# Attention and SwiGLU on one core: 7-for-8 block products for q, k and v, two-bank PSUM tiles, an accumulating residual and a planned engine order

## The chip, the cores and the metric

The kernel runs on one core of one Trainium2 chip. The metric is the device time of an execution in microseconds, as the median over runs. A core has TensorE (PE, matrix products into PSUM), VectorE (DVE), ScalarE (ACT), GpSimd (POOL) and SyncE (SP); the last three issue the transfers here.

## The reference, cut to what matters

S = 2048 rows, D = 1024, F = 3584, 32 heads of 32, all in bf16. Every row attends to 8 rows: itself and those 2, 4, ... 14 before it.

```python
xn  = layernorm(x)
q, k, v = split(xn @ wqkv)                       # [2048, 3 * 1024]
idx = pos[:, None] - 2 * arange(8)               # window 8, dilation 2
a   = softmax(where(idx >= 0, einsum(q, k[idx]) * 32**-0.5, -1e9))
s   = einsum(a, v[idx]).reshape(S, D) @ wo
g   = silu((silu(xn @ w1) * (xn @ w3)) @ w2)
return x + s * g
```

## The kernel before, in words

The rows go in two blocks b of 1024, each of two chunks c of 512; chunk c lies in half c % 2 of `xT` (the normalized rows, transposed, 8 tiles of 128 features by 512 rows) and of `qo` (q, later the attention output). One matmul multiplies a 128x128 weight tile with 128x512 and adds into one PSUM bank of 512 fp32 columns. All products go through `mm_prod` (L117), so that they carry line L120 in the profile and are told apart by the tile they write: qkv, ua / ue / ub (mlp_up), da / de / db (mlp_down), s (wo).

The stages of one block:

- `ln_transpose` (L191): loads x, layernorm, 32 transposes per chunk on TensorE (L182), evictions to `xT`.
- `qkv(c)` (L198): for each of q, k, v 2 MB of weights in two loads (L207) and 8 x 8 matmuls; ScalarE evicts each bank (L220), k and v into `kT` and `vT`, which hold one chunk and the 16 rows before it.
- `xn_sums` (L289): four sums of blocks of `xT`, kept in `xs`.
- `mlp_up` (L335): 14 blocks fb of 256 columns of w1 and w3. Gate and up of both chunks form a 2x2 block product, made with 7 block multiplications in place of 8 (7 x 2 x 4 = 56 matmuls per fb). It takes sums of weight blocks (`w_sums`, L326, made by VectorE in block 0, stored in `s_dram` and loaded again in block 1) and sums of partial products: `fork` (L128) copies a PSUM bank to another, `snap` (L134) copies one to SBUF, and VectorE adds (L374, L383) and multiplies (L397, L400). The last of the seven products is put off into the next fb as `tail` (L393), which `flush` runs.
- `attention(c)` (L229): on VectorE. For each window offset w q*k in two products of 128x2048 (L236), adds over feature groups (L238 to L240) into `E`; 32 transfers of 64 KB by GpSimd regroup E into `L` (L244); softmax in fp32 (L248 to L261); 32 transfers spread the weights over E again (L264); then PV (L272 to L287): products with `vT` and adds into the same half of `qo`.
- `mlp_down(b)` (L425): again a 2x2 block product with 7 multiplications, 392 matmuls; h sums s1 to s4 by VectorE (L463, L464, L478, L490), w2 sums (`w2_sums`, L411, made beside mlp_up of block 0) from `t_dram`.
- `wo(c)` (L525): 64 matmuls; per 128x512 piece a load of x (L538), product with the gate (L541), add (L542), and a store from ScalarE's queue (L543).

The driver (L545) orders them: for each b `qkv(c0)`, in block 1 then `wo(1)`, `xn_sums`, `mlp_up` over the first 11 (block 1: 10) fb, `attention(c0)`, `qkv(c1)`, the other fb, `attention(c1)`, `mlp_down`, `wo(c0)`; `wo(3)` comes last. Within it the framework sets each engine's order by program order, `tc.high_priority()` around operations that free banks, and `tc.issue_after` (L324), which holds weight sums behind a given operation. Pools give the buffers: 8 PSUM banks of [128, 512], `k2` with 8 slots, `r8` with 6 slots for weights, `att` with 3. SyncE's queue carries every load, GpSimd's the stores to scratch and the regrouping.

Of the kernel before, what the change touches and what calls it, by code (L numbers as in the profile page):

```python
# [2 lines left out]

# [5 lines left out]
FP32 = mybir.dt.float32  # L9
# [4 lines left out]
AX = mybir.AxisListType  # L14


@with_exitstack
def kernel(
# [49 lines left out]
    const = ctx.enter_context(tc.tile_pool(name="const", bufs=1))  # L68
    dram = ctx.enter_context(tc.tile_pool(name="dram", bufs=1, space=bass.MemoryType.DRAM))
    psum = ctx.enter_context(tc.tile_pool(name="psum", bufs=8, space=bass.MemoryType.PSUM))  # L70
    small = ctx.enter_context(tc.tile_pool(name="small", bufs=4))
    keep = ctx.enter_context(tc.tile_pool(name="keep", bufs=1))
    r8 = ctx.enter_context(tc.tile_pool(name="r8", bufs=6))
    att = ctx.enter_context(tc.tile_pool(name="att", bufs=3))
    k2 = ctx.enter_context(tc.tile_pool(name="k2", bufs=8))

    s_dram = dram.tile([FB, P, 4, KH, 2 * P], FP16, name="s_dram")
    t_dram = dram.tile([P, FH, 4, CH], FP16, name="t_dram")

# [29 lines left out]

    warm = k2.tile([P, CH], BF16, tag="k2", name="warm")  # L110
    nc.vector.memset(warm[:], 0.0)
    for i in range(8):
        wps = psum.tile([P, CH], FP32, tag="mm", name=f"warm{i}")
        for _ in range(2 if i < 4 else 1):
            nc.tensor.matmul(wps[:], lhsT=warm[:, 0:P], rhs=warm[:], start=True, stop=True)

    def mm_prod(ps, lhs, rhs, first):  # L117
        n = len(lhs)
        for k in range(n):
            nc.tensor.matmul(  # L120
                ps[:], lhsT=lhs[k], rhs=rhs[k], start=(first and k == 0),
                stop=(k == n - 1), skip_group_check=not first,
            )

    def bank(name):
        return psum.tile([P, CH], FP32, tag="mm", name=name)

    def fork(name, src):  # L128
        dst = bank(name)
        with tc.high_priority():  # L130
            nc.scalar.copy(out=dst[:], in_=src[:])  # L131
        return dst

    def snap(name, src):  # L134
        dst = k2.tile([P, CH], FP32, tag="k2", name=name)
        with tc.high_priority():
            nc.scalar.copy(out=dst[:], in_=src[:])
        return dst

    def ln_norm(c, sts, xt4):  # L140
        n = len(sts)
        mv = small.tile([P, n, nc.vector.BN_AGGR_DIM], FP32, tag="mv")
        rstd = small.tile([P, n], FP32, tag="rstd")
        for i, st in enumerate(sts):
            g = c * NST + st
            nc.sync.dma_start(out=xt4[:, st, :], in_=x_flat[g * P:(g + 1) * P, :])
            stats = small.tile([P, 2, nc.vector.BN_STATS_DIM], FP32, tag="stats")
# [11 lines left out]
    def ln_norm_act(c, sts, xt4):  # L159
        n = len(sts)  # L160
        v = small.tile([P, 4, n], FP32, tag="v")
# [8 lines left out]
        with tc.high_priority():  # L170
# [424 lines left out]
```

## Time and profile before

| | us |
|---|---|
| median of 3 runs (766.59 to 772.36) | 768.1 |
| span of the profiled execution | 766.9 |
| TensorE busy | 749.4 |
| VectorE busy | 602.1 |
| ScalarE busy | 321.1 |
| GpSimd busy | 97.2 |

The busy time of each engine in each stage, from the profile's table of windows (PE and DVE in us, DMA the mean busy share of the 16 DMA engines):

| window, us | stage | PE | DVE | DMA |
|---|---|---|---|---|
| 0 to 13.1 | layernorm and transposes of chunk 0 | 8.28 | 7.27 | 0.86 |
| 13.1 to 57.2 | qkv(0), transposes of chunk 1 | 44.10 | 28.26 | 0.59 |
| 57.2 to 190.8 | mlp_up(0), 11 fb, attention(0) | 133.28 | 117.67 | 0.79 |
| 190.8 to 239 | qkv(1) | 43.80 | 47.92 | 0.59 |
| 239 to 276.1 | mlp_up(0), 3 fb | 36.85 | 34.38 | 0.62 |
| 276.1 to 365.2 | mlp_down(0), attention(1) | 88.84 | 44.55 | 0.69 |
| 365.2 to 379 | wo(0) | 13.80 | 11.12 | 0.90 |
| 379 to 434.2 | qkv(2), wo(1) | 55.20 | 54.37 | 0.55 |
| 434.2 to 561.7 | mlp_up(1), 10 fb, attention(2) | 124.17 | 99.23 | 0.56 |
| 561.7 to 602 | qkv(3) | 40.30 | 32.20 | 0.40 |
| 602 to 650.7 | mlp_up(1), 4 fb | 48.70 | 39.59 | 0.59 |
| 650.7 to 735.1 | mlp_down(1), attention(3) | 84.40 | 59.59 | 0.56 |
| 735.1 to 767 | wo(2), wo(3) | 27.66 | 25.95 | 0.38 |

How to read it: the page's first part says which engine could bound the whole, its slices show where it does not work, the chain says what the end followed from, and the groups say what one operation lasts and what it waited for. Durations of one engine's neighbours overlap, so that the cost of one more operation is the distance between starts, which the timeline and the chain of work show. Transfers are given by line with the median from issue to landing.

### The profile page before, as it was taken

The page shows a single profiled execution, that of the slowest core. Times are in us where ns is not written, and L with a number is a line of the kernel's source. Part 1 is how long each engine was busy: PE and PEld are TensorE (multiplying, and loading weights), DVE is VectorE, ACT ScalarE, POOL GpSimd, SP SyncE. Part 2 cuts the span into 40 slices and gives each one's busy share as a digit, 9 for nine tenths or more (in the row PEclk, how much of TensorE's full clock was granted, in tenths as well). Part 3 has the DMA queues.
Part 4 walks back from the last instruction along what each step waited for, and adds up shares of the span by engine and source line. Part 5 has one row for each costly group of instructions (what it writes and reads, how often), then busy time and mean ns, then how long its engine had stood idle before and what let it go on. Part 6 is the DMA issues. An engine that isn't in the chain of part 4 may idle for free.

```text
span 766.9 us, 9404 instructions
## 1 busy us (share of the span) xinstructions
PE 749.4 (98%) x3516; PEld 375.6 (49%) x3516; DVE 602.1 (79%) x828; ACT 321.1 (42%) x534; POOL 97.2 (13%) x172
## 2 busy tenths in 40 slices
PE   7999999999899999999999899999999999999997
PEld 4664444444565444445566344444466544444443
DVE  6479988887998999150799998565995995924997
ACT  5536444654225489264033044464433444321200
POOL 0000042132000001413000004040000004040000
PEclk8999999999999999999999999999999999999999
DMA  9633799898753668658853836565535257464634
GB/s 331 217 111 108 234 302 272 275 285 297 261 189 83 218 227 268 172 190 262 261 179 103 270 114 169 175 195 165 187 115 201 98 172 207 157 196 147 200 100 140
DMA packets 123117, 150.56 MB, mean 196 GB/s; under 512 B 6080, under 2 KB 97728, under 8 KB 119488
## 3 DMA queue, kind: packets, MB, share of 16 engines
q1 hardware_dynamic: 110336, 115.36, 48.2%
q0 software_dynamic: 8128, 30.42, 11.7%
q10 hardware_dynamic: 4608, 4.20, 1.6%
q8 instruction: 27, 0.44, 0.3%
q14 instruction: 18, 0.15, 0.1%
HBM read 115.34 MB, written 26.21 MB: 185 GB/s over the span
## 4 chain that ended last, share of the span: by engine, by line
PE 86%; DVE 8%; DMA 4%; issue 1%; ACT 1%; SPq 0%; DVEq 0%; ACTq 0%
PE ub L120 18%; PE qkv L120 15%; PE ue L120 12%; PE ua L120 12%; PE db L120 9%; PE de L120 6%; PE da L120 6%; PE s L120 5%; DMA wt<-in_A_wqkv_dram 2%; DVE B L286 1%; DVE B L272 1%; DVE qo L287 1%; DVE p_t L236 1%; PE tp L182 1%; DVE C L272 1%
## 5 line engine op out<-in xcount | busy, mean ns | idle before, releaser
L120 PE MATMUL qkv<-xT,wt 128*128 128x512 bf16 x768 | 169.9, 383 | 4.9 <-DMA wt<-in_A_wqkv_dram 4.4
L120 PEld LDWEIGHTS <-wt 128*128 128x128 bf16 x768 | 110.1, 144 | 63.8 <-DMA wt<-in_A_wqkv_dram 5.8
L120 PEld LDWEIGHTS <-st 128*128 128x128 f16 x896 | 87.7, 98 | 107.4 <-issue 1.7
L120 PE MATMUL ua<-xT,w 128*128 128x512 bf16 x448 | 106.7, 381 | 2.9 <-ACT ub L131 2.9
L120 PEld LDWEIGHTS <-w 128*128 128x128 bf16 x672 | 65.9, 98 | 84.0 <-issue 5.9
L120 PE MATMUL ub<-xs,st 128*128 128x512 f16 x448 | 106.7, 381 | 0.0
L120 PEld LDWEIGHTS <-h_sb 128*128 128x128 bf16 (+1 forms) x672 | 65.5, 98 | 77.5 <-issue 0.5
L236 DVE TENSOR_TENSOR p_t<-qo,kT 128x2048 bf16<-128x2048 bf16 x64 | 77.5, 1215 | 8.5 <-ACT kT L220 8.5
L120 PE MATMUL db<-wt,h_sb 128*128 128x512 f16 x336 | 73.7, 379 | 0.0
L374 DVE TENSOR_TENSOR us<-ue,us 128x512 f32<-128x512 f32 x56 | 37.5, 685 | 38.3 <-PE ue L120 38.3
L120 PE MATMUL s<-wot,qo 128*128 128x512 bf16 x256 | 55.7, 379 | 0.0
L367 ACT ACTIVATE h_sb<-ua 128x512 bf16<-128x512 f32 x56 | 33.3, 598 | 53.3 <-PE ua L120 53.3
L385 ACT ACTIVATE sg<-us 128x512 bf16<-128x512 f32 x56 | 34.8, 630 | 46.7 <-DVE us L374 46.7
L120 PE MATMUL ub<-xs,w 128*128 128x512 f16 x224 | 53.4, 379 | 0.9 <-DVE h_sb L383 0.9
L120 PE MATMUL ue<-xs,st 128*128 128x512 f16 x224 | 52.9, 379 | 0.1
L120 PE MATMUL ue<-xT,st 128*128 128x512 bf16 x224 | 52.9, 379 | 0.0
L131 ACT COPY ub<-ua 128x512 f32<-128x512 f32 x56 | 31.6, 570 | 44.4 <-PE ua L120 25.4
L120 PE MATMUL da<-wt,h_sb 128*128 128x512 bf16 x224 | 49.2, 379 | 0.3 <-DMA wt<-in_B_w_dram 0.3
L264 POOL DMA_DIRECT2D E<-pb x64 | 36.8, 582 | 92.9 <-DVE pb L261 89.1
L397 DVE TENSOR_TENSOR h_sb<-h_sb,ub 128x512 bf16<-128x512 bf16 x56 | 37.0, 679 | 14.4 <-PE ub L120 14.4
L244 POOL DMA_DIRECT2D L<-E x64 | 37.0, 586 | 59.3 <-DVE E L240 55.6
L220 ACT CAST qo<-qkv 128x512 bf16<-128x512 f32 x32 | 18.6, 585 | 61.3 <-PE qkv L120 45.0
(103 smaller groups left out, 841.1 us busy)
## 6 DMA issues: line engine op xcount, KB each, us to landing
wt<-in_A_wqkv_dram SPq DMA_DIRECT2D x24, 1024.0 KB, 7.1
w<-in_B_w_dram SPq DMA_DIRECT2D x42, 512.0 KB, 5.1
s_dram<-st POOLq DMA_DIRECT2D x14, 1024.0 KB, 5.9
wt<-t_dram SPq DMA_DIRECT2D x16, 896.0 KB, 5.4
st<-s_dram SPq DMA_DIRECT2D x14, 1024.0 KB, 5.3
wt<-in_B_w_dram SPq DMA_DIRECT2D x12, 896.0 KB, 6.1
wot<-in_A_wo_dram SPq DMA_DIRECT2D x8, 1024.0 KB, 7.9
w2q<-in_B_w_dram SPq DMA_DIRECT2D x14, 512.0 KB, 3.8
```

The source lines that it names most:

```text
L120: nc.tensor.matmul(ps[:], lhsT=lhs[k], rhs=rhs[k], start=(first and k == 0), stop=(k == n - 1), skip_group_check=not first,)
L131: nc.scalar.copy(out=dst[:], in_=src[:])
L182: nc.tensor.matmul(tp[:, k * P:(k + 1) * P], lhsT=xt4[:, st, kt * P:(kt + 1) * P], rhs=ident[:], start=(k == 0), stop=(k == KH - 1), skip_ ...
L220: nc.scalar.copy(out=dst, in_=ps[:])
L236: nc.vector.tensor_mul(p_t[:], qT[:, jh * 4:jh * 4 + 4, :], kT[:, jh * 4:jh * 4 + 4, o:o + CH])
L244: nc.gpsimd.dma_start(out=L[r // 2][sq * 32:(sq + 1) * 32, r % 2, :, :], in_=E[r:P:NR, :, sq * P:(sq + 1) * P],)
L264: nc.gpsimd.dma_start(out=E[r:P:NR, :, sq * P:(sq + 1) * P], in_=pb[sq * 32:(sq + 1) * 32, :, :],)
L272: nc.vector.tensor_mul(dst, E[:, w, :].unsqueeze(1).to_broadcast([P, 4, CH]), vT[:, js, o:o + CH])
L367: nc.scalar.activation(out=h_sb[:, fl[i], 0:CH], in_=pa[i][:], func=ACTF.Silu)
L374: m = nc.vector.tensor_add(su2[i][:], pe[i][:], su2[i][:])
L385: nc.scalar.activation(out=sg2[i][:], in_=su2[i][:], func=ACTF.Silu)
L397: nc.vector.tensor_mul(h_sb[:, fl[i], 0:CH], h_sb[:, fl[i], 0:CH], pb[i][:])
```

## The change

1. *7 for 8 in q, k, v.* `group`, taken out of `mlp_up`, is used by `pair` for k and v in block 0 and for q, k and v in block 1, over both chunks at once; q of block 0 stays plain. Sums of the weights (`pair_sums`) are four VectorE operations of 128x2048 per matrix; those of k and v are stored in `sk_dram` and loaded again in block 1. The second chunk's k and v wait in `kv_dram` (block 0) or in `h_sb` (block 1, `park`) and are moved into `kT` and `vT` by GpSimd transfers once attention of the first chunk has used them. It is for fewer matmuls and for reading wqkv once per block.
2. *Two-bank tiles.* PSUM tiles become [128, 2, 512], four of them, and `k2` has 4 slots of twice the size; evictions, silus, adds and products take 1024 columns at once. The w2 sums are made two blocks at a time.
3. *Attention's regrouping through DRAM.* E goes to `e_dram` in two halves and comes back in 4 transfers each; p goes to `p_dram` in 4 transfers per half and returns with one that repeats each row 4 times. The z sums go by halves, and PV takes window offsets 0 to 3 for both feature halves, then 4 to 7.
4. *The residual.* `residual(c)` copies x to the output from DRAM to DRAM on SyncE's queue, ahead of the load of fb 6 of block 0. The wo pieces (128x1024) are multiplied with the gate in fp32, and GpSimd adds them to the output with an accumulating transfer. The last two pieces are done as before.
5. *wo(0) and the transposes of chunks 2 and 3 inside mlp_down(0)*: pieces of either follow single products of its last two multiplications.
6. *A planned order.* `Plan` reads the finished program, gives every instruction and transfer a cost, list-schedules them forward and backward six times, and adds order-only dependencies, so that VectorE, ScalarE and GpSimd run in the order planned; TensorE and SyncE keep the program's. `tc.high_priority` and `tc.issue_after` go.
7. *The driver*: see the end of the diff; CUT is (13, 10), so that attention(0) follows fb 12, and attention(1) fb 13.

The diff's core (`Plan`'s methods, mlp_down's evictions and the changes of names and pools left out):

```diff
+    def group(nm, a11, a12, a22, s, c11, c12, c22, c21):
+        s1, s2, s3, s4 = s
+        pa = bank(f"ua{nm}")
+        for i in I:
+            mm_prod(pa[:, i], a11[i], b11, True)
+        pe = bank(f"ue{nm}")
+        for i in I:
+            mm_prod(pe[:, i], s1[i], t1, True)
+        pb = fork(f"ub{nm}", pa)
+        sp5 = snap(f"us5{nm}", pe)
+        flush()
+        for i in I:
+            mm_prod(pa[:, i], a12[i], b21, False)
+        c11(pa)
+        for i in I:
+            mm_prod(pb[:, i], s2[i], t2, False)
+        su2 = snap(f"us2{nm}", pb)
+        for i in I:
+            mm_prod(pe[:, i], s4[i], b22, False)
+        c12(pe, su2)
+        for i in I:
+            mm_prod(pb[:, i], s3[i], t3, False)
+        c22(pb, sp5)
+
+        def tail():
+            for i in I:
+                mm_prod(pb[:, i], a22[i], t4, False)
+            c21(pb)
+        pend.append(tail)
...
+            def second(ps, part, js):
+                if later is None:
+                    nc.vector.tensor_add(d1[:, js, :], ps[:], part[:])
+                else:
+                    kv = k2.tile([P, 2, CH], BF16, tag="k2", name=f"kv{b}_{t}_{js.start}")
+                    nc.vector.tensor_add(kv[:], ps[:], part[:])
+                    nc.gpsimd.dma_start(out=kv_dram[later, :, js, :], in_=kv[:])
...
+        def gather(wh):
+            ws = slice(wh * 4, wh * 4 + 4)
+            nc.gpsimd.dma_start(out=e_dram[wh], in_=E[:, ws, :].rearrange("p w t -> p (w t)"))
+            for sq in range(4):
+                nc.gpsimd.dma_start(
+                    out=L[wh][sq * 32:(sq + 1) * 32],
+                    in_=e_dram[wh].rearrange("(h r) (w q t) -> h (r w) q t", r=NR, w=4, q=4)[:, :, sq, :],
+                )
...
+            if direct:
+                for i in I:
+                    nc.vector.tensor_mul(o_t[:, i], ps[:, i], gg[:, i])
+                    nc.vector.tensor_add(x_e[:, 1, i], o_t[:, i], x_e[:, 0, i])
+                    nc.scalar.dma_start(out=orow[:, i], in_=x_e[:, 1, i])
+            else:
+                nc.vector.tensor_mul(o_t[:], ps[:], gg)
+                nc.gpsimd.dma_start(out=orow, in_=o_t[:], accum_op=ALU.add)
...
+    def residual(c):
+        rows = slice(c * CH, (c + 1) * CH)
+        nc.sync.dma_start(out=out_flat[rows, :], in_=x_flat[rows, :])
...
+    plain(0, 1, qo[:, 1], wq, range(NJ))
+    pair(1, 0, wk, sk, kd, None, 0)
+    pair(2, 0, wv, sv, vd, None, 1)
+    w2_load(0)
+    mlp_up(0, range(5))
+    for c in range(2 * NB):
+        residual(c)
+    mlp_up(0, range(5, CUT[0]))
+    attention(0, kv_dram[0], kv_dram[1])
+    mlp_up(0, range(CUT[0], FB))
+    attention(1)
+    mlp_down(0)
+    xn_sums()
+    parks = {0: (None, park(2)), 1: (park(3), park(5)), 2: (park(4), park(6))}
+    for t in (0, 1, 2):
+        w_t = wqkv_load(t, f"w{'qkv'[t]}1")
+        s_t = pair_sums(t, 1, w_t, t > 0)
+        d0, d1 = parks[t]
+        pair(t, 1, w_t, s_t, qo[:, 0] if t == 0 else d0, d1)
+    wo(1)
+    move(kT, park(3))
+    move(vT, park(4))
+    nc.gpsimd.dma_start(out=qo[:, 1], in_=park(2))
+    mlp_up(1, range(10))
+    attention(2, park(5), park(6))
+    mlp_up(1, range(10, FB))
+    attention(3)
+    mlp_down(1)
+    wo(2)
+    wo(3, last=2)
+
+    plan.enforce(nc, tc)
```

## The prediction

> **What bounds the kernel now.** I read the engine table first, then the chain that ended last, then TensorE's waits, then VectorE's timeline. The page's engine table and its slices of clock and DMA:
>
> ```profile
> PE 749.4 (98%) x3516; PEld 375.6 (49%) x3516; DVE 602.1 (79%) x828; ACT 321.1 (42%) x534; POOL 97.2 (13%) x172
> ...
> PEclk8999999999999999999999999999999999999999
> DMA  9633799898753668658853836565535257464634
> ...
> PE 86%; DVE 8%; DMA 4%; issue 1%; ACT 1%; SPq 0%; DVEq 0%; ACTq 0%
> ```
>
> TensorE is busy 98% at full clock, and the chain is TensorE's own for 86%: time leaves only if matmuls leave or a hole closes. The price of a matmul is its spacing, not the 379 to 383 ns duration (instructions overlap). The chain in order of time (start us, us, what) gives it:
>
> ```profile
> 29.77 27.64 PE qkv L120 x128
> 57.40 1.73 PE ua L120 x8
> ...
> 188.35 6.11 DMA wt<-in_A_wqkv_dram
> ...
> 440.79 2.76 PE ua L120 x8
> ...
> 735.14 27.64 PE s L120 x128
> ```
>
> 27.64 / 128 = **0.2159 us**, and 1.7266 / 8 = 0.2158 from neighbouring starts. 3516 matmuls are 3376 of 128x512, 128 transposes (32 in 1.79 us, 0.056 each) and 12 warm-ups. After the first product at 13.08 come 3376 x 0.2158 + 96 x 0.056 = 734.0 us, but the last ends at 762.8: 15.7 us are holes. TensorE's waits (total, times, longest) name some:
>
> ```profile
> PE qkv L120 <- DMA wt<-in_A_wqkv_dram: 4.4, 3, 3.5
> PE ua L120 <- ACT ub L131: 2.9, 1, 2.9
> PE ub L120 <- DVE h_sb L383: 0.9, 3, 0.4
> ```
>
> The qkv wait is followed by 83 matmuls in 19.8 us in place of 17.9, and the ub wait by 8 in 2.76 us in place of 1.73: each long wait costs a further 1.7 to 1.9 us of slow matmuls. So qkv(c1) costs 6.6, the start of block 1 4.9, scattered pieces 4.
>
> VectorE comes next: by the table of windows it is busy 117.7 of 133.6 us between 57.2 and 190.8. Its timeline (start, duration) gives cadences:
>
> ```profile
> 444.98 0.68 DVE L239 TENSOR_TENSOR p_t<-p_t 128x1024 bf16<-128x1024 bf16 x1
> 445.58 1.22 DVE L236 TENSOR_TENSOR p_t<-qo,kT 128x2048 bf16<-128x2048 bf16 x1
> 446.72 0.42 DVE L240 TENSOR_TENSOR E<-p_t 128x512 bf16<-128x512 bf16 x1
> 447.06 0.69 DVE L374 TENSOR_TENSOR us<-ue,us 128x512 f32<-128x512 f32 x1
> 447.67 1.22 DVE L238 TENSOR_TENSOR p_t<-p_t 128x2048 bf16<-128x2048 bf16 x1
> 448.80 0.68 DVE L374 TENSOR_TENSOR us<-ue,us 128x512 f32<-128x512 f32 x1
> ```
>
> Start to start: 1.14 us for 2048 bf16, 0.60 for 1024, 0.34 for 512, 0.61 for 512 with fp32 or PSUM. An operation that reads the result just ahead starts 0.12 later (another L238 of 2048 at 468.62, the L239 on its result at 469.87: 1.25).
>
> [...]
>
> **The change, part by part.**
>
> *Products.* k and v of block 0 and q, k, v of block 1 go from 128 matmuls per chunk to 112: five matrices x 16 = 80 fewer, 80 x 0.2158 = **17.3 us off TensorE**, all on the path. Gap-free it then needs 734.0 - 17.3 = 716.7 us after the first product. Both chunks are made together, so the qkv(c1) stages and their loads vanish and with them the 6.6 us hole; the weights of q, k, v are read once per block (12 MB in all, not 24). The 4.9 us hole sits between wo(1) and the first up group; the new order has q/k/v pairs, then wo(1) with loads issued ahead, so I count it gone.
>
> *VectorE work.* Added: 12 sums of 2048 (12 x 1.14 = 14) and 20 PSUM adds of 1024 (23). Removed: 24 of 32 residual adds (24 x 0.61 = 15), and the fixed part of every merged pair: no 1024 PSUM operation is in the trace. It costs at most two of 512, 1.22; the nearest row, the softmax's fp32 subtraction of 1024 (L255), lasts 1226 ns, so 1.15 start to start, as durations exceed cadences by 0.08 here. I take 1.15: 0.07 saved per pair, with four pairs (three on PSUM) x 28 groups 8 us. 602 + 37 - 23 = 616 us, 100 under TensorE's 717: no bound over the whole, only by stage.
>
> *Fixed order and mlp_down(0).* The list fixes VectorE's order. After block 13's c22 add it runs: one 512-pair multiply, 8 sums of 1792 (1.0 each), ten PV operations of attention(0) (11.8), and only then block 13's tail multiply. The second product of mlp_down(0) needs that multiply 16.4 us after block 13's s3 product (76 matmuls), VectorE delivers 23.6 after: **7.2 us** of stall. To the add that frees the bank for the x2 transposes VectorE has 80 operations, 78.1 us by these cadences, against 71.1 us of TensorE: also 7, so the one stall covers both. In `up` groups it is just in time (slack 2 us of 12). I add 1.7 us of slow clock: **8.9**. Bounds: 5 (shorter operations, no slow clock) to 11.
>
> *Residual copies.* Four 1 MB DRAM-to-DRAM copies enter the SyncE queue near 134 us, ahead of w0_6's load. No row shows such a copy. Least: 4 MB at the 312 GB/s that this queue does when busy (115.4 MB in 48.2% of 767) is 13 us; most: read and write both counted, 27. w0_6 then lands 17 to 30 us later than 134, i.e. 151 to 164; its sums stand first in VectorE's order at 151, and TensorE needs them at 163 with some 2 us of slack. TensorE loses 0 to 14 us. I take **4**, since 16 engines were only 79% busy there and the other queues share them. That stage also gains 9 MB (copies, k/v park, attention's trips), so DMA is nearly full: another **1** for small waits.
>
> *Attention trips.* E and p go through DRAM: 20 issues in place of 32 per chunk at 0.58 us each, GpSimd saves 7 us per chunk off the path. The second half of z waits for a write and a read in turn (about 4.5 + 4.6 us) against 5.5 us of other VectorE work: 3 to 4 us of VectorE idle per chunk, hidden by TensorE's work except as included above (attention(3) ends about 9 us ahead of wo(3)).
>
> *ScalarE, kv moves, transposes, wo(0) woven into mlp_down.* Nothing: ScalarE is idle 58%, merging saves it time; the moves are 1 MB on GpSimd's queue (5.9 us for s_dram's stores) with 20 us or more until use.
>
> *Ends.* Start: 13.1 before; splitting the transposes' evictions may add up to 1 on VectorE: 14.1. Tail: before, last matmul to end of span 4.1. Now the last direct piece's x load waits for a slot freed by an accumulate, issued 10 us before the end. [...] tail 4.1 to 8, I take 5.
>
> Sum: 14.1 + 716.7 + 8.9 + 4 + 1 + 5 = **749.7** span; the runs' median is 1.2 above the profile's span (768.1 against 766.9): **751 us**.
>
> **Rivals.**
> (a) *TensorE stays fed.* The stalls are absorbed (PV operations shorter than counted, copies at full rate): 13.1 + 716.7 + 3 + 4.2 + 1.2 = 738 us. For: 98% busy now, the holes have named causes that the edit removes. Against: the order puts ten PV operations ahead of a needed multiply whatever the data.
> (b) *The copies block the queue.* w0_6 14 us late plus 1.7 of slow clock, tail 8: 751 + 11.7 + 3 = 766 us, no change (within 1% of 768). For: one queue, served in order, DMA already at 9 tenths in those slices. Against: copies can share 16 engines at 79%.
> (c) *The other side: the fixed order amplifies late transfers.* A late L, E or accumulate now holds everything queued behind it on VectorE: the PV multiplies and up adds that TensorE waits for. Before, the same late arrivals cost VectorE 16.2 us (E) and 6.8 (L). If half of the 23 repeat on TensorE's path with (b)'s loss and five slow-clock periods of 1.7: 766 + 11.5 + 8.5 = 786, slower. Against: attention has whole up groups between producer and user.
>
> **How the numbers follow.** Chances: forecast band 0.58, (a) 0.22, (b) 0.11, (c) 0.09. Predicted is the likeliest, 751. From the forecast down: stall 5 for 8.9, no copy loss, tail 4.1 make 742, and the start's 1 us and the small waits' 1 make 740, from where (a) takes over; from it up: (b) at 766. I set 739 to 765: (c), the half of (a) under 739 and the top of (b) are the 2 in 10 left out. Faster by over 1% (under 760.4): the forecast, (a) and a little of (b): 0.82. Same: 0.10. Slower: 0.08.
>
> **What would show it.** TensorE at 3436 matmuls with 0.2158 spacing and busy near 730; no qkv waits for weights between 180 and 240; one wait of about 7 us of the second product of mlp_down(0) for the tail multiply near 275 to 282; a wait for w0_6's sums near 150 to 165 with copies taking 13 to 27 us from 134; VectorE 600 to 616; tail 4 to 8. Wrong if matmul spacing changes with two-bank tiles, if accumulates or DRAM trips take over 10 us, or if the holes close altogether.

## The result, and the profile after

The changed kernel takes **777.9 us** (median; 775.7 to 783.6) against 768.3 us (766.6 to 772.4) for the kernel before: a ratio of 1.0124 with a 95% interval of 1.0079 to 1.0170, 1.2% slower. The forecast was 751 us, 2.2% faster. A second set of runs of the changed kernel, beside other experiments, gave 779.5 us and 1.0129 (1.0079 to 1.0179). Ratios here and below leave out executions in a slower state; only prio2 had any, four of its 20.

The page of the changed kernel, its engine table, clock, DMA share and the chain's shares:

```profile
PE 731.3 (94%) x3378; PEld 355.5 (46%) x3436; DVE 629.0 (81%) x694; ACT 294.2 (38%) x314; POOL 96.7 (12%) x150
...
PEclk7999999998999998999999999999999999999999
DMA  9294267998888752756777458983743667565626
...
PE 73%; DMA 11%; DVE 9%; issue 4%; POOL 1%; ACT 1%; SPq 0%; DVEq 0%; POOLq 0%
```

TensorE's busy time fell by 18 us, as 80 matmuls at 0.2158 us should make it fall (17.3). But the span is 9 us longer, TensorE is at 94% in place of 98%, and transfers and VectorE hold 20% of the chain in place of 12%. (58 of the 3436 matmul records are missing here, so the count tells nothing.) TensorE's waits in the changed kernel (engine, line, what it waited for; total, times, longest):

```profile
PE ub L399 <- DVE h_sb L741: 8.6, 3, 4.5
PE tp L453 <- DVE x L428: 7.8, 3, 4.4
PE da L399 <- DVE h_sb L749: 7.3, 1, 7.3
PE ue L399 <- DVE h_sb L749: 6.1, 2, 4.4
PE s L399 <- DMA wo<-in_A_wo_dram: 1.5, 1, 1.5
```

The waits for qkv weights and for the fork are gone, as expected. In their place almost every wait is for VectorE. (The transposes `tp` wait at the start.) To add up what each wait costs, with the slow matmuls after it, I took the start of each product in the timeline and subtracted its place in a stream without gaps (0.2158 us per matmul, 0.056 per transpose). The growth of that difference is TensorE's loss, by stage, in us:

| | before | after |
|---|---|---|
| first product starts at | 13.1 | 17.4 |
| losses to the end of the q/k/v stage of block 0 | 0.9 | 2.5 |
| mlp_up(0) | 8.0 | 12.4 |
| mlp_down(0), first half | 0.4 | 9.0 |
| wo(0) pieces, transposes, q/k/v of block 1 | 0.2 | 3.3 |
| start and rest of block 1 | 5.9 | 8.3 |
| last matmul to the end | 4.1 | 5.9 |

(For before, mlp_up(0) includes qkv(1).) For after, 17.4 + 716.7 of unbroken stream + 35.5 of losses + 5.9 = 775.5, the profile's span of 775.7. Four places matter.

**The copies.** SyncE's and then VectorE's timeline of the changed kernel (start, duration, what ended the idle time before it):

```profile
142.03 2.54 SPq L947 DMA_DIRECT2D out_dram<-in_A_x_dram  x4
149.74 0.37 SPq L704 DMA_DIRECT2D w<-in_B_w_dram  x1
150.16 7.05 SPq L706 DMA_DIRECT2D w<-in_B_w_dram  x1
```

```profile
156.65 1.23 DVE L741 TENSOR_TENSOR h_sb<-ub,us 128x1024 bf16<-128x1024 f32 x1 [0.43 <-PE ub L399]
170.07 0.69 DVE L513 TENSOR_TENSOR st<-w 128x1024 f16<-128x1024 bf16 x1 [12.19 <-DMA w<-in_B_w_dram]
...
173.55 1.21 DVE L749 TENSOR_TENSOR h_sb<-h_sb,ub 128x1024 bf16<-128x1024 bf16 x1
```

The copies are issued from 142 on and have landed by 160.4. Fb 6's load, issued behind them at 150, lands 19.8 us later, at 170. VectorE stands before the weight sums for 12.2 us, and the tail multiply at 173.55, which frees a bank that TensorE waits for, is queued behind them. TensorE loses 10.9 us from here to 187.

**mlp_down(0).** VectorE and TensorE of the changed kernel around 300 us:

```profile
288.40 2.35 DVE L675 TENSOR_TENSOR att<-E,vT 128x2048 bf16<-128x2048 bf16 x2
...
297.99 2.35 DVE L675 TENSOR_TENSOR att<-E,vT 128x2048 bf16<-128x2048 bf16 x2
300.26 1.22 DVE L749 TENSOR_TENSOR h_sb<-h_sb,ub 128x1024 bf16<-128x1024 bf16 x1
```

```profile
301.53 10.93 PE L399 MATMUL da<-r,h_sb 128*128 128x512 bf16 x43 [7.34 <-DVE h_sb L749]
```

Ten PV operations from 288.4 on, then the multiply, then the second product: the wait that was predicted, 7.34 us (7.2 predicted).

**Attention(2)** in VectorE's timeline of the changed kernel:

```profile
518.21 0.69 DVE L649 TENSOR_TENSOR z<-z,L 128x512 f32<-128x512 f32 x1
528.39 0.69 DVE L647 TENSOR_TENSOR z<-L 128x512 f32<-128x512 bf16 x1 [9.49 <-DMA L<-e_dram]
529.00 1.21 DVE L749 TENSOR_TENSOR h_sb<-h_sb,ub 128x1024 bf16<-128x1024 bf16 x1
...
534.24 1.22 DVE L733 TENSOR_TENSOR us<-ue,us 128x1024 f32<-128x1024 f32 x1
535.37 1.22 DVE L741 TENSOR_TENSOR h_sb<-ub,us 128x1024 bf16<-128x1024 f32 x1
```

The second half of z waits 9.5 us for its way through DRAM, a write to e_dram and a read into L. The chain of the changed kernel (start, duration, what):

```profile
511.06 7.34 DMA e_dram<-E
...
520.84 7.53 DMA L<-e_dram
```

Three operations that free TensorE's banks (L749, L733, L741) stand behind that z sum. TensorE loses 8.1 us by 542.

**The start** loses 4.3 us against before (experiment start_free).

### The profile page after: what moved, and what is told of

It reads as the page before. It is cut to its first block, busy times and chain, and to the rows that moved or that the text cites. A ratio compares the mean times of both kernels' runs of the same rounds, so it can differ in the third digit from the quotient of the medians.

```text
span 775.7 us, 8625 instructions
## 1 busy us (share of the span) xinstructions
PE 731.3 (94%) x3378; PEld 355.5 (46%) x3436; DVE 629.0 (81%) x694; ACT 294.2 (38%) x314; POOL 96.7 (12%) x150
## 4 chain that ended last, share of the span: by engine, by line
PE 73%; DMA 11%; DVE 9%; issue 4%; POOL 1%; ACT 1%; SPq 0%; DVEq 0%; POOLq 0%
PE ub L399 14%; PE ue L399 9%; PE ua L399 9%; PE db L399 8%; PE ubq L399 6%; PE de L399 6%; PE da L399 5%; PE s L399 4%; DMA w<-in_B_w_dram 4%; PE qkv L399 4%; PE ueq L399 4%; PE uaq L399 4%; DMA e_dram<-E 2%; DMA L<-e_dram 2%; DVE att L675 1%
## 5 line engine op out<-in xcount | busy, mean ns | idle before, releaser
L399 PEld LDWEIGHTS <-h_sb 128*128 128x128 f16 (+1 forms) x800 | 80.3, 101 | 99.7 <-DVE h_sb L749 7.8
L635 DVE TENSOR_TENSOR att<-qo,kT 128x2048 bf16<-128x2048 bf16 x64 | 76.0, 1219 | 9.5 <-ACT kT L595 5.0
L399 PE MATMUL db<-r,h_sb 128*128 128x512 f16 x336 | 73.7, 379 | 0.1
L675 DVE TENSOR_TENSOR att<-E,vT 128x2048 bf16<-128x2048 bf16 x56 | 66.8, 1219 | 0.0
L399 PE MATMUL s<-wo,qo 128*128 128x512 bf16 x249 | 55.9, 379 | 1.8 <-DMA wo<-in_A_wo_dram 1.5
L399 PE MATMUL da<-r,h_sb 128*128 128x512 bf16 x218 | 50.2, 387 | 7.6 <-DVE h_sb L749 7.3
L733 DVE TENSOR_TENSOR us<-ue,us 128x1024 f32<-128x1024 f32 x28 | 34.2, 1222 | 11.9 <-PE ue L399 11.4
L741 DVE TENSOR_TENSOR h_sb<-ub,us 128x1024 bf16<-128x1024 f32 x28 | 34.2, 1222 | 8.1 <-PE ub L399 8.1
L637 DVE TENSOR_TENSOR att<-att,att 128x2048 bf16<-128x2048 bf16 x32 | 39.1, 1223 | 0.8
L749 DVE TENSOR_TENSOR h_sb<-h_sb,ub 128x1024 bf16<-128x1024 bf16 x28 | 34.0, 1216 | 3.7 <-PE ub L399 3.7
```

What stands on the lines that cost most here:

```text
L399: nc.tensor.matmul(ps, lhsT=lhs[k], rhs=rhs[k], start=(first and k == 0), stop=(k == n - 1), skip_group_check=not first,)
L635: nc.vector.tensor_mul(p_t[:], qT[:, jh * 4:jh * 4 + 4, :], kT[:, jh * 4:jh * 4 + 4, o:o + CH])
L637: nc.vector.tensor_add(pr[0][:], pr[0][:], pr[1][:])
L675: nc.vector.tensor_mul(dst, E[:, w, :].unsqueeze(1).to_broadcast([P, 4, CH]), vT[:, jh * 4:jh * 4 + 4, o:o + CH])
L733: nc.vector.tensor_add(su2[:], pe[:], su2[:])
L741: nc.vector.tensor_add(h_sb[:, fl, CH:BL], pb[:], sp5[:])
```

## The experiments

Each was timed beside the kernel before on the same chip; that kernel's median was 769.9 to 771.3 us in these sets, so ratios are what to compare. The changed kernel's is 1.0124. Losses are counted as above, from each run's own profile.

### First set: one place at a time

**copies_early.** The order on all engines but SyncE was kept.

```diff
     sv = pair_sums(2, 0, wv, False)
+    for c in range(2 * NB):
+        residual(c)
...
     mlp_up(0, range(5))
-    for c in range(2 * NB):
-        residual(c)
```

> Only the place of the four residual copies on SyncE's queue changes: behind the loads of v's weights (about 50 us) in place of ahead of fb 6's load (142 us). The order on every other engine is that of the changed kernel. Theory A (the copies stand in the queue ahead of fb 6's load, and VectorE's fixed order waits for it): the 12.2 us wait of the weight sums and the 10.9 us that TensorE falls behind between 174 and 187 us vanish, about 767 us in place of 777.9, and the load lands within 6 to 8 us of its issue in place of 19.8. Rival B (the DMA engines are full there whoever asks, 9 tenths in those slices): the load still takes over 12 us and TensorE still loses over 6 us, 773 us or more.

Measured: 776.9 us, ratio 1.0083 (1.0053 to 1.0112), an interval that overlaps the changed kernel's: by the total rival B's outcome. But fb 6's load landed 6.3 us after its issue and the loss after it fell from 10.9 to 2.4 us, so the copies were its cause. TensorE now lost 6.2 us at 67 to 73 instead. VectorE's timeline of copies_early shows why:

```profile
61.69 0.69 DVE L781 TENSOR_TENSOR w2q<-w2q 128x1024 f16<-128x1024 bf16 x1 [14.67 <-DMA w2q<-in_B_w_dram]
...
64.48 1.22 DVE L596 TENSOR_TENSOR kv<-ueq,us2q 128x1024 bf16<-128x1024 f32 x1
65.61 1.21 DVE L596 TENSOR_TENSOR kv<-ubq,us5q 128x1024 bf16<-128x1024 f32 x1
```

The w2 load now stands behind the copies, and the planned order has the w2 sums, which nobody needs before mlp_down, ahead of the kv adds that free PSUM banks. Neither theory foresaw this: the delay moved to another load, which again had needed work queued behind it.

**tail_first.**

```diff
     def enforce(self, nc, tc):
...
-        for x in sorted(range(len(insts)), key=lambda x: (start[x], x)):
+        for x in self.shift(insts, sorted(range(len(insts)), key=lambda x: (start[x], x))):
```

(`shift` moves block 13's tail multiply, L749, behind the last of the s3 sums.)

> One VectorE instruction moves: block 13's tail multiply runs ahead of the ten PV operations that stood before it. Theory A (its place in the fixed order is the cause of the 7.3 us wait of the second product of mlp_down(0), with 1.6 us of slow matmuls after it): 9 us less, about 769 us. Rival B (the prediction's count: VectorE has 78 us of work against 71 of TensorE's up to the add that frees the bank of the x2 transposes): the stall only moves there, a wait of about 7 us for a sum of the last products at about 340 us, and no more than 2 us are won, 776 us.

Measured: 783.3 us, ratio 1.0168 (1.0132 to 1.0204). The wait for the multiply went, and these came in its place (TensorE's waits of tail_first):

```profile
PE da L406 <- ACT db L413: 3.1, 1, 3.1
PE db L406 <- DVE h_sb L851: 2.5, 1, 2.5
```

ScalarE had the fork of the second bank (303.9 us) queued behind 20 us of layernorm statistics for chunks 2 and 3, and VectorE the s2 sums behind the same PV operations. The loss in mlp_down(0) is 9.1 us as before. That the stall moves was rival B's forecast, though neither place was the one it named.

**z_late.**

```diff
-        tree(zm, z, nc.vector.tensor_max)
-        nc.vector.tensor_sub(z[:], z[:], zm[:, 0:1, :].to_broadcast([P, W, P]))
+        zo += tree(zm, z, nc.vector.tensor_max)
+        zo.append(nc.vector.tensor_sub(z[:], z[:], zm[:, 0:1, :].to_broadcast([P, W, P])))
+        if c == 2:
+            plan.late = {o.ins.name for o in zo}
```

(In the planned order these operations go behind the c22 add of fb 3 of block 1.)

> In attention(2) the second half of the z sums, the max tree and the subtraction (7 VectorE operations) move behind the three operations of the up groups that were queued after the first of them. Theory A (the z sum waits 9.5 us for its trip through DRAM, and the multiply and the add that free TensorE's banks stand behind it): the 4.5 us wait at 531 us and most of the 8.1 us that TensorE falls behind between 527 and 541 us vanish, about 770 us. Rival B (the lateness of the trip is only handed on to softmax, PV or a later up group): under 3 us won, 775 us or more, with a new wait after 541 us.

Measured: 783.9 us, ratio 1.0173 (1.0136 to 1.0211). ScalarE's timeline of z_late has the answer:

```profile
539.42 1.06 ACT L667 ACTIVATE z<-z 128x1024 f32<-128x1024 f32 x1 [7.61 <-DVE z L664]
...
541.79 1.06 ACT L747 ACTIVATE sg<-us 128x1024 bf16<-128x1024 f32 x1
542.75 1.01 ACT L412 COPY ub<-ua 128x1024 f32<-128x1024 f32 x1
```

The softmax's exponential waits for the moved operations, and the fork that TensorE needs stands behind it on ScalarE: a wait of 6.0 us for `ub`, 8.7 us lost in all, as much as before. Lateness was handed to the next fixed queue.

**start_free.**

```diff
-        for x in sorted(range(len(insts)), key=lambda x: (start[x], x)):
+        for x in sorted(range(self.free, len(insts)), key=lambda x: (start[x], x)):
...
+    plan.free = len(list(nc.cur_bb.bb.instructions))
     plain(0, 0, qo[:, 0], wq, range(6))
```

> The planned order is imposed only from chunk 0's first product on; ahead of it the framework's own order stands. Theory A (VectorE and ScalarE work off the layernorm of chunk 0 in an order planned with wrong times; the statistics of the later tiles stand behind evictions): the first product starts at 13 to 14 us in place of 17.4, about 773.5 us. Rival B (the later rows of x land late, or the split evictions set the start): it starts at 16.5 us or later, 777 us.

Measured: 778.5 us, ratio 1.0102 (1.0059 to 1.0145). TensorE's timeline of start_free:

```profile
12.95 2.29 PE L399 MATMUL qkv<-xT,wq 128*128 128x512 bf16 x5 [0.67 <-ACT xT L460]
```

Theory A holds for the start: 12.95 us in place of 17.43. But the whole is no faster: TensorE lost 5.9 us more at 200 to 212, where VectorE stood 7.8 us before the weight sums of fb 8 for a load that landed 15.4 us after its issue. The same late load (15.4 to 15.5 us) appears in the profiles of tail_first, z_late and less_dve (6.6 to 7.3 us of VectorE's time), and not in that of the changed kernel (10.9 us, 2.9 of VectorE's time). Tail_first and z_late change nothing ahead of 280 us, so their edits did not make that load late; what did is not shown.

### Second set: is it the order, its times, or the work?

**after_again.** The changed kernel, no edit.

> The changed kernel once more, beside the others of this call. In three of the four experiments TensorE fell behind by another 4 to 6 us at 205 to 215 us, which the profile of the changed kernel does not show. If that loss comes with the copies in most executions, the median is 779 to 783 us here too; if it came from the edits, 776 to 778.

Measured: 779.5 us (775.9 to 782.2), ratio 1.0129. Its profile has 11.2 us lost after the copies and no late load at 205. The median lies just inside the first expectation; executions 6 us apart (775.9 and 782.2) fit a late load that is sometimes there, but no more than that is shown, for neither profile of this kernel has one.

**prio.**

```diff
-    plan.enforce(nc, tc)
...
     def fork(name, src):
         dst = bank(name)
-        nc.scalar.copy(out=dst[:], in_=src[:])
+        with tc.high_priority():
+            nc.scalar.copy(out=dst[:], in_=src[:])
```

(and so for the other operations that had this priority before.)

> The planned order is taken out; the framework's own order stands, with the priorities that the kernel before gave to evictions, forks, adds and sums (attention fills in). All work is the same. Theory A (the fixed order hands every late transfer and every misjudged time on to TensorE: start 4.3, after the copies 11 to 16, mlp_down(0) 9, attention(2) 8): at most 760 us, first product at about 13 us, the wait in mlp_down(0) under 2 us. Rival B (the work itself is too much for VectorE and the DMA engines in block 0, in whatever order): 773 us or more, with TensorE as far behind at the end of mlp_down(0).

Measured: 789.8 us, ratio 1.0271 (1.0220 to 1.0323). The first product starts at 12.7, and mlp_down(0) loses 0.8 us: two losses of the planned order are its own. But the copies and what follows cost 18 us, and a new wait appears (TensorE's waits of prio):

```profile
PE ueq L399 <- DVE sk L518: 12.6, 1, 12.6
```

The q sums of block 1 had no priority, and VectorE made them among PV operations of attention(1). So theory A's two details were right, and its sum of at most 760 us was wrong. Rival B's came closer: the total is over 773 us, and up to the x2 transposes in mlp_down(0) TensorE has lost 22 us after its first product, 24 in the changed kernel. That this is not the amount of work, as B has it, only the last set shows; here another order has other places that lose.

**measured.**

```diff
-                edges[x, len(res)] = (1.3 if res[x] == "Pool" else 0.9) - dur[x]
+                edges[x, len(res)] = (2.0 if res[x] == "Pool" else 1.3) - dur[x]
...
-                    edges[moved[d], x] = 1.1 + self.LAG
+                    edges[moved[d], x] = 2.2 + self.LAG
...
-                    edges[d, x] = 0.0 if res[d] == res[x] else self.TAIL[res[d]]
+                    edges[d, x] = (0.12 if res[d] == "DVE" else 0.0) if res[d] == res[x] else self.TAIL[res[d]]
```

(ScalarE's costs and the transfers' rates, which also change, are left out here.)

> The planner stays, with times nearer to the traces: transfers land 1.1 us later and start 0.4 to 0.7 later, move 15% slower (DRAM to DRAM half as slow again), a VectorE operation on the result just ahead costs 0.12 us more, ScalarE's 0.03 to 0.05 more. Theory A1 (a planned order is fine, its times were wrong): 765 us or less, the waits in mlp_down(0) and at attention(2) mostly gone. Rival A2 (an order fixed ahead cannot follow transfers that take 5 us once and 20 us another time): 774 us or more, waits in other places.

Measured: 786.2 us, ratio 1.0220 (1.0182 to 1.0259). Attention(2) lost nothing at 530, but mlp_down(0) lost 17.8 and fb 12 of block 1 13.5 us. Rival A2's outcome.

**down_first.**

```diff
-            nc.vector.tensor_sub(s2t[g], s1t[g], a11[g])
+            m = nc.vector.tensor_sub(s2t[g], s1t[g], a11[g])
+            if b == 0:
+                plan.ahead(m, 17 + g)
```

(`ahead` moves an operation so many places forward on its engine: also the tail multiply 10, the last s4 sum 8, the two adds of each half 10, the first wo product 6, ScalarE's second fork 11.)

> Planned order as in the changed kernel, but in mlp_down(0) VectorE's tail multiply, s2 and s4 sums, the adds that free banks and the first wo product go 6 to 20 VectorE operations ahead of where they were, past attention operations alone, and ScalarE's second fork goes ahead of most of the layernorm statistics of chunks 2 and 3. Theory A (order alone causes the 9 us of mlp_down(0); the earlier experiment failed since the same PV operations also stood ahead of the s2 sums, and the statistics ahead of the fork): TensorE loses under 2 us between 275 and 365 us, 8 us less than the run of the changed kernel beside it. Rival B (VectorE has 78 us of work against 71 of TensorE's, and attention(1) is then late by as much): the loss comes back at wo(0), at the first sums of block 1 or at wo(1), under 3 us won.

Measured: 784.5 us, ratio 1.0208 (1.0157 to 1.0260). The second product of mlp_down(0) no longer waited. But TensorE lost 6.6 us at 338, before the x2 transposes, and 9.2 at the wo(0) pieces (TensorE's waits of down_first):

```profile
PE tp L466 <- DVE o L956: 7.6, 1, 7.6
...
PE de L410 <- ACT dsp L424: 4.8, 1, 4.8
```

The wo product (L956) stood behind a z sum of attention(1), which waited 9.9 us for L. Rival B's outcome; whether by its cause, too much work, is left open here, for the wait that ended last was one for a transfer.

### Third set: the amount of work, the copies, the trips

**less_dve.**

```diff
-        nc.vector.tensor_sub(tq[:, :, 0], bq[:, :, 1], bq[:, :, 0])
+            nc.vector.tensor_sub(tq[:, :, 0, n], bq[:, :, 1, n], bq[:, :, 0, n]),
```

(n is 8 columns, in all four sums.)

> Leaves out most of the w2 sums (each of the 28 VectorE operations works on 8 of 512 columns, so that mlp_down's products are of other numbers); orders, loads and stores are those of the changed kernel. VectorE has some 16 us less work between 120 and 260 us. Theory D (in block 0's mlp_up and mlp_down VectorE's work of 234 us and its waits for transfers of 33 us exceed the 245 us that TensorE needs there): TensorE's loss between 97 and 366 us, 21 us in the changed kernel, falls by 8 us or more, 770 us or less. Rival O (late transfers and places in the order alone, each wait being local): the losses after the copies (11), at fb 11 (1) and in mlp_down(0) (9) stay as they are, 776 us or more.

Measured: 782.7 us, ratio 1.0166 (1.0122 to 1.0210). VectorE is busy 614.7 us in place of 629.0, 14 less, and nothing was won: mlp_down(0) lost 9.3 us, attention(2) 8.7, and the copies and fb 8's late load 14.3. **13 us less work for VectorE from 120 to 260 us (97.3 us busy in place of 110.5), in the same order, win no time.** Theory D falls, though VectorE's share of the stages (193.0 of the 224.0 us from 190 to 414 in the changed kernel, 86%, beside 211.5 of TensorE) looked like a bound. The work inside mlp_down(0) itself was not reduced.

**spread_start.**

```diff
+            if 1 <= fb <= 8:
+                residual(8 * b + fb - 1)
...
-    def residual(c):
-        rows = slice(c * CH, (c + 1) * CH)
+    def residual(r):
+        rows = slice(r * P, (r + 1) * P)
```

(The start is free as in start_free, and the order is planned anew.)

> The residual copies in 16 pieces of 256 KB, each behind one fb's loads (chunks 0 and 1 in block 0, 2 and 3 in block 1), planned anew, and the start in the framework's order. Theory A (a queue of 4 MB ahead of one load is what hurts): the 11 us after the copies vanish, with the start's 4.3 us: 763 to 766 us. Rival B (VectorE's order hands any delay on, and the start's gain is used up further on, as it was when the start alone was freed): 772 us or more.

Measured: 769.8 us (20 runs), ratio 0.9989 (0.9972 to 1.0007). First product at 13.1, 4.8 us lost after the copies in place of 10.9 to 17; mlp_down(0) still 9.3, attention(2) 10.3. Between the two expectations: A's mechanism, less of its gain. Fb 6's load still took 16.0 us to land, and in the new order GpSimd's 1 MB move of kT and the first e_dram write go beside it (148.8 and 153.1 us, 174.1 and 179.2 in the changed kernel); VectorE's wait for it was 5.5 us in place of 12.2.

**attold.**

```diff
-            nc.gpsimd.dma_start(out=e_dram[wh], in_=E[:, ws, :].rearrange("p w t -> p (w t)"))
...
+            for r in range(NR):
+                for sq in range(4):
+                    nc.gpsimd.dma_start(
+                        out=L[wh][sq * 32:(sq + 1) * 32, r], in_=E[r:P:NR, ws, sq * P:(sq + 1) * P],
+                    )
```

(p's way back is changed in the same manner. The kernel before had 16 transfers each way per chunk, half of the 32 that its description gives; here there are 32 of half the size.)

> Attention's regrouping as in the kernel before, SBUF to SBUF in transfers of 32 KB by halves of the window (64 per chunk each way in all in place of 20), planned anew. Theory A (the two-step trip through DRAM, 7.3 + 7.5 us at attention(2), makes VectorE wait): VectorE's waits for L and E, 19 to 27 us in the changed kernel, halve, and the 8 us at attention(2) go: 770 us or less. Rival B (64 issues of 0.58 us per chunk on GpSimd take as long as the trip): the waits stay or grow, 778 us or more.

Measured: 782.4 us, ratio 1.0165 (1.0119 to 1.0210). VectorE's waits for L total 26 us in place of 19, and GpSimd is busy 188 us in place of 97: by the total and by these waits rival B's outcome. Losses at attention(2) fell to 2.7 us and in mlp_down(0) to 2.1, but the new plan lost 8.9 us in the k/v stage and 17.7 after the copies. As the plan was made anew, how much of each difference is the trip's can't be told.

**prio2.** The edit of prio, the copies of spread_start, and:

```diff
-            sums(st, wa, wb, 0, 1)
+            with tc.high_priority():
+                sums(st, wa, wb, 0, 1)
```

> No planner; the framework's order with the priorities of the kernel before, now also for the q sums of block 1 (their lateness cost 12.8 us in the run without the planner), and the copies in 16 pieces. All else is the changed kernel's. Theory A (without the planner mlp_down(0) loses 0.8 us in place of 9 and the start 0; what was left, the copies' 11 us and the q sums' 13 to 17, has causes of its own): 789.8 - 11 - 15 = 764 us. Rival B (VectorE is full in block 0 and the losses come back at the next needed operation): 780 us or more.

Measured: 773.9 us over all 20 runs (765.4 to 777.8), ratio 1.0010 (0.9987 to 1.0034). The q sums' wait shrank from 12.6 to 1.6 us and the losses from 52 to 32 us. Neither theory's number: losses of 0.5 to 7 us remained in a dozen places, the largest at the start (5.8), at 186 to 198 (7.2) and at 228 to 240 us (5.8).

### Fourth set: a plan whose transfers land later

What was left: single repairs moved the wait, less work won nothing. Does a planned order lose this time with any times, or because its transfers land later than planned?

**late_only.**

```diff
-                    edges[moved[d], x] = 1.1 + self.LAG
+                    edges[moved[d], x] = 2.7 + self.LAG
...
-            return n / 1200 + (0.055 if ps else 0.1) + (0.19 if len(list(ins.outs)) > 1 else 0)
+            return n / 1200 + (0.135 if ps else 0.18) + (0.19 if len(list(ins.outs)) > 1 else 0)
```

> The changed kernel, planned with two other numbers alone: a transfer's data are there 1.6 us later, and each ScalarE operation takes 0.08 us more (the traces have 5.3 to 7.5 us from issue to landing for L and e_dram where the plan has some 3 to 4). Theory A1 (the order is good for the times it was planned with; transfers that land later than planned make VectorE stand before its next operation): the 9 us in mlp_down(0) and the 8 us at attention(2) shrink by half or more, the copies' 11 us stay: 768 to 772 us. Rival A2 (a fixed order loses this time somewhere with any times; the run with all times measured lost 17.8 and 11.8 us in two places): 776 us or more.

Measured: 779.8 us, ratio 1.0106 (1.0079 to 1.0132). By the total this is rival A2's outcome; by the stages it is half A1's: mlp_down(0) lost 1.9 us in place of 9.0, attention(2) still 8. The copies' loss had grown to 23 us. The chain of late_only in that stretch (start, duration, what):

```profile
148.09 0.39 SPq L704
148.48 0.04 issue
148.53 32.58 DMA w<-in_B_w_dram
```

GpSimd's timeline there has the move of kT at 144.6 and the first e_dram write at 151.9: attention's own transfers met the copies. Loads of this kind took 6.3 us with neither beside them (fb 6 in copies_early), 12.9 with attention's transfers (fb 8 there), 19.8 with the copies, and 32.6 here with both. The orders differ in more than that, so it is a pattern and no proof.

**late_spread.** The edits of spread_start and of late_only together.

> The same two numbers in the plan, together with the copies in 16 pieces and the free start (769.8 us with the plan's own numbers). Theory A1: 12 us or more below that, 753 to 758 us, no wait of TensorE's over 4 us between 100 and 700 us. Rival A2: 766 us or more, the losses of mlp_down(0) and attention(2), 9 and 10 us there, back at other operations.

Measured: 758.1 us, ratio **0.9828** (0.9797 to 0.9860). mlp_down(0) loses 0.7 us, the copies 4.4; attention(2) still 8.3 (one wait of 5.4 us, so that part of A1's expectation failed). The total lies at the upper end of A1's range.

**late11.** As late_spread, and in addition:

```diff
-    mlp_up(1, range(10))
+    mlp_up(1, range(11))
     attention(2, park(5), park(6))
-    mlp_up(1, range(10, FB))
+    mlp_up(1, range(11, FB))
```

> As the run beside it, with attention(2) put after fb 11 of block 1 in place of fb 10, so that its transfers have one group more before a wo product or a move needs them. Theory A1: 748 to 756 us, faster than the kernel before by over 1.5%. Rival A2: as the run beside it or slower, 766 us or more.

Measured: **753.1 us** (752.2 to 753.9), ratio **0.9760** (0.9734 to 0.9786): faster than both kernels. Page and TensorE's waits of late11:

```profile
PE 730.1 (97%) x3436; PEld 353.9 (47%) x3436; DVE 626.8 (83%) x694; ACT 296.2 (39%) x316; POOL 95.6 (13%) x150
```

```profile
PE tp L453 <- DVE x L428: 2.8, 1, 2.8
PE ub L399 <- DVE h_sb L743: 2.7, 3, 1.2
PE ua L399 <- DVE h_sb L751: 2.2, 1, 2.2
```

VectorE and TensorE are busy within 2.2 us of what they were in the changed kernel, and the span is 24 us shorter: that the same work can be ordered so is the answer to prio's rival B and to theory D. In late11's timeline six PV operations stand ahead of the tail multiply in mlp_down(0) in place of ten, and the second product waits 0.2 us for it. 13.8 + 716.7 + 13.6 of losses + 7.4 of tail = 751.5 (span 751.6). Losses in the runs that tell the story, in us:

| | first product at | after the copies, to 220 us | mlp_down(0), first half | rest of block 1 | ratio |
|---|---|---|---|---|---|
| changed kernel | 17.4 | 10.9 | 9.0 | 8.3 | 1.0124 |
| less_dve | 17.9 | 14.3 | 9.3 | 8.7 | 1.0166 |
| spread_start | 13.1 | 4.8 | 9.3 | 10.3 | 0.9989 |
| late_only | 15.0 | 23.1 | 1.9 | 8.1 | 1.0106 |
| late_spread | 12.8 | 4.4 | 0.7 | 10.2 | 0.9828 |
| late11 | 13.8 | 6.2 | 0.7 | 3.5 | 0.9760 |

What is shown: edits of the copies' place and size (copies_early, spread_start), of the start's order (start_free), of the plan's two times for mlp_down(0) (late_only, late_spread) and of attention(2)'s place (late11) move the losses that they were aimed at. These four columns hold 21.4 of the 24.1 us of span between the changed kernel and late11; the small waits gave another 4.2, and a longer tail took 1.5. In late11 attention(2)'s stage loses 1.0 us in place of 8.2, and mlp_down(1) now 2.5. What is not shown: whether the 1.6 us or the 0.08 us of ScalarE did it, for both were changed together; how much of late11's last 5 us is the group more and how much the new order that came with it; and why the plan of `measured`, with 1.1 us on the landing and five other times changed, did worse. The planner answers small changes of its times with quite different orders, so one order's success is no proof that its times are the right ones.

## Why the prediction was wrong

Its sum was 749.7 us of span; measured were 17.4 (start) + 716.7 (stream) + 9.0 (mlp_down(0)) + 10.9 (copies) + 15.6 (small waits and attention(2)) + 5.9 (tail). No one term carries the difference of 26 us. The largest, attention(2)'s 8.3, was put at nothing; the copies (by 6.9), the small waits (6.3) and the start (3.3) were sized too small.

- **Products: right.** The spacing is 0.2158 us with two-bank tiles too (chain pieces of 1.73 us for 8), TensorE is busy 18 us less, the weight waits of qkv(1) are gone, and so is the 4.9 us hole ahead of block 1's first up group (1.3 us are lost at block 1's q product instead). The 128 and 112 matmuls stand for a matrix and two chunks, not for one chunk; the 80 are right.
- **VectorE's work: 13 us short** (616 against 629), with no consequence that less_dve could find. The count of residual adds was also off: 28 of 32 went, not 24, since the two direct pieces keep four, so that the sum should have been 2.4 us lower and the shortfall larger. What the rest is was not traced. A 1024 PSUM operation costs 1.13 us from start to start (534.24 to 535.37), as taken.
- **mlp_down(0): right in size** (7.34 us of wait and 9.0 of loss against 7.2 and 8.9) and in the operations named. The second reason given beside it, 78 us of VectorE's work against 71, was not tested as such; a plan made with two other times removed the loss with the same work (late_only). The multiply's place was right as the cause of this wait, but not the only thing late there: when it went ahead, as much was lost at the next late operations (tail_first).
- **The residual copies: mechanism right, term mis-sized.** All four had landed 18.3 us after the first was issued and the load 28 us after it, inside the 13 to 27 and 17 to 30 worked out; but 4 us was taken from a span of 0 to 14, with the argument that the DMA engines were only 79% busy. It was 10.9. Rival (b)'s "served in order" is shown for the landings alone: those of SyncE's 192 transfers before, and of its 158 in the changed kernel, stand in the order of issue. The copies made the load late (copies_early); whether by standing ahead of it in the queue or by keeping the engines busy, no run separates.
- **"Hidden by TensorE's work except as included above": the step that failed.** The trips through DRAM were said to make VectorE wait 3 to 4 us per chunk at no cost. At attention(2) it waited 9.5 us, and TensorE lost 8.1; the stage's 8.3 us is the term put at nothing. "Attention has whole up groups between producer and user" is true of the data, but not of the queue: what TensorE needs next stood behind the waiting z sum on VectorE, or behind the waiting exponential on ScalarE (z_late). The trip of 4.5 + 4.6 us assumed (the medians from issue to landing of the 64 KB transfers before, L<-E and E<-pb) was 7.3 + 7.5. A trip of over 10 us was one of the prediction's own signs of being wrong; three of the 14 accumulates took over 10 us as well (10.8 to 16.0), though no wait of TensorE's is for one of them directly.
- **The start and the small waits: too small.** The start was given 1 us for split evictions; it lost 4.3, and another 2.5 in the q/k/v stage. One microsecond for small waits was 4.8 (1.5 at fb 11, 1.6 for the first wo load, 1.7 in transposes and q/k/v). The start is the plan's order by itself (start_free).
- **Slow matmuls after a wait: right.** TensorE's timeline usually has 1.89 us for 8 matmuls. Before, 8 took 2.76 us after the wait of 2.9 us for `ub`, at a granted clock of 0.67 (440.7 to 443.5 us). In the changed kernel 8 took 3.15 us after a wait of 2.82 (at 181.2, clock 0.57) and 3.57 us after one of 4.48 (at 536.6, clock 0.53), but 1.89 us after one of 1.67 (at 530.3, clock 1.00). After the 7.34 us in mlp_down(0) the clock was 0.50 from 301.5 to 304.
- **The tail: 5.9 against 5.** Its upper bound of 8 was an estimate of the author's. The six accumulates issued from 747 us on landed after 4.5 to 4.8 us; the plain 512 KB stores to t_dram before took 3.7 in the median.

3.3 (start) + 6.9 (copies) + 8.3 (attention(2)) + 6.3 (q/k/v stage and small waits) + 0.9 (tail) = 25.7 of the 26 us between 749.7 and 775.7. The right case was rival (c), "the fixed order amplifies late transfers", which was given 0.09 and a time 8 us too long; its argument against itself, whole up groups between producer and user, is what the queue undid. Before the change VectorE had waited for transfers too (16.2 us for E, 6.8 and 3.8 for L). VectorE's waits before (what it waited for; total, times, longest):

```profile
DVE us L374 <- PE ue L120: 38.3, 28, 3.7
...
DVE qo L272 <- DMA E<-pb: 16.2, 1, 16.2
...
DVE z L248 <- DMA L<-E: 6.8, 1, 6.8
DVE z L249 <- DMA L<-E: 3.8, 1, 3.8
```

The same add on the page of the changed kernel (busy us, mean ns; idle us before it, and for what):

```profile
L733 DVE TENSOR_TENSOR us<-ue,us 128x1024 f32<-128x1024 f32 x28 | 34.2, 1222 | 11.9 <-PE ue L399 11.4
```

Before, VectorE waited 38.3 us for `ue`, that is, it ran ahead of TensorE and had room; in the changed kernel it waited 11.4 us. This is a likely reason why such waits cost nothing then, and it was not tested.

## What to carry to other kernels

When a change makes an engine with a planned order wait for more transfers, cost each wait by what stands behind the waiting instruction on its own engine, not by how much time lies between the producer and the consumer of the data: at attention(2) three operations stood behind a wait of 9.5 us, and TensorE lost 8.1. An order planned ahead depends on its planned landing times, and small changes of them give quite different orders: landing 1.6 us later won (late_spread), 1.1 us later with other changes lost (measured). So measure several. Keep bulk copies in small pieces behind the loads that are due: with 16 pieces of 256 KB TensorE lost 4.8 us after the copies (spread_start), with four of 1 MB 10.9. A wait that moves when one instruction is moved points to the plan; try other times in the plan before repairing place after place.

## What the runs showed of the hardware

- Landing times varied with what else was queued: fb 6's load took 6.3 us without the copies (copies_early), 19.8 us behind them, and 32.6 us in late_only, where GpSimd's kT move and e_dram write met them; fb 8's took 15.4 to 15.5 us in four profiles, 10.9 in that of the changed kernel and 11.3 in after_again's. The median of these 512 KB loads in the changed kernel is 5.4 us.
- Four DRAM-to-DRAM copies of 1 MB issued together landed 8.3, 11.4, 14.3 and 16.4 us after issue.
- In the changed kernel GpSimd took 1.17 to 1.36 us to issue one accumulating transfer of 512 KB in fp32, twice the 0.58 us that is its median for plain ones (0.53 to 0.95); they landed after 6.1 us in the median (4.5 to 16.0). In late11, with its last matmul at 744.2, the tail is 7.4 us; the last direct pieces wait 3.1 us for an accumulate to free a slot.
- A program with 14 us less VectorE work (less_dve) took no less time, and one with the same work to 2.2 us in another order (late11) took 24 us less.
